# Keys and queries turned by VectorE blocks and SBUF transfers instead of TensorE transposes

## The chip, the cores and the metric

The kernel runs on one core of a Trainium2 chip. Its time is the device time of one execution in microseconds, from runs of the whole program. A profiled execution gives a trace beside it: busy times of the engines, what each instruction waited for, and the transfers.

## What is computed

A gated linear recurrence (4 batches, 8 heads, 768 steps, head dimension 48) is followed by a feed-forward block (3072 tokens, 384 to 2048 to 384). Cut to what matters:

```python
# attention: complex gate, real keys, values and queries
mag = np.sqrt(a_re * a_re + a_im * a_im)
scale = np.minimum(mag, 0.999) / (mag + 1e-06)
ar, ai = a_re * scale, a_im * scale
for t in range(S):
    S_re, S_im = (ar[t] * S_re - ai[t] * S_im + outer(k[t], v[t]),
                  ar[t] * S_im + ai[t] * S_re)
    y[t] = q[t] @ S_re
# feed-forward on x = y with heads side by side
h = x @ w_in
sp = np.maximum(h, 0.0) + np.log1p(np.exp(-np.abs(h)))
out = (h * erf(sp)) @ w_out
```

## The kernel before, in words

The 3072 tokens are cut into twelve units of 256 tokens, three to a batch, and each unit into two chunks of 128 tokens. Tokens lie over the 128 partitions. The path that runs is `quotient_path`; a second one, `product_path`, follows only where a check at the end finds a value out of its limits.

For each unit, the gate work (`g_mag` to `g_sin`, mostly ScalarE activations and VectorE arithmetic) makes running decays `pr` and angles `CS`. With these, `prep` multiplies a chunk's keys and queries by their decay and by cosine and sine: the tiles `kt` and `qt`, 128 tokens by 8 heads by 96 numbers (real and imaginary part of 48). The recurrence inside a chunk then becomes matrix products:

- `cols` (line 996) turns `kt` and `qt`, so that the 96 numbers lie over the partitions and tokens along the row. Four heads at a time are transposed on TensorE (line 1001) into PSUM, and a copy (line 1004) by ScalarE or VectorE brings them to SBUF as `kT` and `qT`. A chunk takes 16 transposes and 4 copies.
- `scores` (line 1008) multiplies turned keys by turned queries, a product of 96 by 128 by 128 for each head, and masks the result to the tile `A`.
- `state` (line 1019) makes the state for the next chunk from `kt`, not turned, and the values.
- `xT` (line 1038) adds, for each head, `A` times values and turned queries times the state (line 1060), four blocks of 32 columns side by side.

The result, turned already, goes into the feed-forward block: `ff_in` (line 1080), the activations `softplus` (line 726) and `erf_times_h` (lines 1107 to 1111), and `ff_out_8` or `ff_out_7` (lines 1140 and 1178).

Each engine works off one queue in program order. The order is written by hand: every step has a due time in units in the table `WHEN`, all steps of all units stand in one list `plan`, and the list is sorted by due time and emitted. So the work of one unit's attention stands between matmuls of the unit before it. Ten numbers, `st`, place the ten steps of a chunk. All transfers of this part but two are issued on SyncE's queue, SP: loads of gates, keys, queries and values, the weights, the outputs, and small ones that carry a row (`wrow` and `w` in `g_decay`, a row of `F` in `g_angle`). An issue on SP waits there for what its transfer needs, and later issues wait behind it.

Tiles come from pools with a set number of buffers: `kT` has two, `qT` three, `kt` and `qt` one each. A tile with one buffer is written again only when its last reader is done.

Of the kernel before, what the change touches and what calls it, by code (L numbers as in the profile page):

```python
# [35 lines left out]
def weave(*streams):  # L36
# [5 lines left out]
    for _, _, _, step in sorted(order, key=lambda e: e[:3]):  # L42
# [1 line left out]

WHEN = {'qact': 3,
 'a00': [0.385, 0.699, 0.3, 0.31, 0.32, 0.33, 0.569, 0.34, 0.35, 0.63],
 'a01': [0.526, 0.422, 0.611, 0.637, 0.649, 0.542, 0.659, 0.66, 0.67, 0.681],
 'n': [0.676, 0.782, 0.769, 0.972, 1.105, 1.183, 1.312, 1.472, 1.61, 1.914, 1.96, 2.139, 2.151, 2.632, 2.395],  # L50
 'g1': [0.702, 0.752, 0.792, 0.802, 0.835, 0.842, 0.873],
 'att': {1: [[0.931, 1.297], 1.089], 2: [[1.716, 2.133], 1.029], 3: [[3.038, 3.627], 1.205]},
 'gate': {2: [1.212, 1.259, 1.372, 1.391, 1.423, 1.442, 1.362], 3: [1.508, 1.606, 1.912, 2.106, 2.59, 2.234, 2.172]},
 'hps': {0: [[0.767, 0.876], [1.01, 1.426]],
         1: [[1.778, 2.017], [2.342, 2.684]],
         2: [[3.136, 3.262], [3.538, 3.868]],
         11: [[11.97, 12.371], [12.438, 12.72]]},
 'act': {0: [2.6, 2.924],
         1: [3.328, 3.7],
         2: [4.148, 4.4],  # L60
         3: [4.9, 5.2],
         4: [5.752, 6.098],
         10: [11.679, 12.031],
         11: [12.456, 12.882]},
 'ops': {0: [3.021, 3.377, 3.704],
         1: [4.001, 4.639, 4.84],
         2: [4.452, 4.798, 4.884],
# [1 line left out]
         10: [12.146, 12.41, 13.01],  # L69
         11: [12.97, 13.469, 14.216]},  # L70
 'T': 5.125,
 'gr': [-1.569, -1.419, -1.119, -0.953, -0.478, -0.129, -1.279],
 'st': [0.014, 0.03, 0.059, 0.09, 0.12, 0.15, 0.206, 0.25, 0.281, 0.388],
 'hr': [1.113, 1.509, 1.573, 1.938],
 'ar': [1.472, 1.947],
 'or': [2.163, 2.683, 3.173],
# [4 lines left out]
 'rest': 12.3,  # L81
 'ok': 13.7,
 'al': [[11.145, 11.515], [11.266, 11.738]],
 'qone': 0,
 'c1g': [0.36, 0.37, 0.38],
 'warm': 0.335}

# [526 lines left out]
def quotient_path(  # L614
# [62 lines left out]
    make_identity(nc, ident)  # L677
    triu = const.tile([P, P], FP, name="triu")
    make_upper_triangular(nc, triu, val=1.0, diag=True)
    cold = tmp.tile([P, P], FP, tag="m", name="cold")  # L680
    vector.memset(cold, 0.0)
    ones = const.tile([P, 1], FP, name="ones")
    vector.memset(ones, 1.0)
# [201 lines left out]
    def g_mag(u, cc=ALL):  # L885

        ar, ai = gate(u, cc)
        s, y = t_("s", cc), t_("y", cc)
        T["s", u] = T["s"]
        i = u * C + cc[0]  # L890
        T["kept"] = u == 1
        act(out=s, in_=ar, func=AF.Square, accum_out=large[:, i:i + 1])
        act(out=y, in_=ai, func=AF.Square)
        T["kept"] = False
        vector.tensor_tensor(out=s, in0=s, in1=y, op=OP.add)
# [14 lines left out]
    def g_log(u, cc=ALL):  # L910
        s, y = T["s"][:, cc[0]:cc[1]], T["y"][:, cc[0]:cc[1]]
        act(out=s, in_=s, func=AF.Ln)
        act(out=y, in_=s, func=AF.Exp, scale=-0.5)
        act(out=y, in_=y, func=AF.Ln, scale=EPS, bias=1.0)
        vector.tensor_scalar(out=s, in0=s, scalar1=0.5, scalar2=math.log(CAP), op0=OP.mult, op1=OP.min)
        T["logs"] = vector.tensor_tensor(out=g_("lr", u, cc), in0=s, in1=y, op=OP.subtract)

    def g_turn(u, cc=ALL):
        th = T["th", u][:, cc[0]:cc[1]]
# [2 lines left out]
    def g_angle(u, c):  # L922

        th = T["th", u][:, c, :]
        goes_on = u % PER > 0 or c > 0
        on_pe = u < PER
        if goes_on:
            prev = T["F", u][:, c - 1, :] if c > 0 else T["F", u - 1][:, C - 1, :]
            if not on_pe:
                row = T["s", u][0:1, c, :]  # L930
                nc.sync.dma_start(out=row, in_=prev[P - 1:P, :])
                vector.scalar_tensor_tensor(out=th[0:1, :], in0=row, scalar=TAU, in1=th[0:1, :],
                                               op0=OP.mult, op1=OP.add)
        ps = ps_b.tile([P, DM], FP, tag="b", name="sum")
        nc.tensor.matmul(out=ps, lhsT=turns, rhs=th, start=True, stop=not (goes_on and on_pe))
        if goes_on and on_pe:
            nc.tensor.matmul(out=ps, lhsT=ident[:, P - 1:P].to_broadcast([P, P]), rhs=prev, start=False, stop=True)
        F = g_("F", u, (c, c + 1))[:, 0, :]
        vector.tensor_scalar(out=F, in0=ps, scalar1=MAGIC, scalar2=MAGIC, op0=OP.add, op1=OP.subtract)
        vector.tensor_tensor(out=F, in0=ps, in1=F, op=OP.subtract)  # L940
# [40 lines left out]
    def chunk(u, c):  # L981
# [5 lines left out]
        def prep(nm, e):  # L987
# [5 lines left out]
                st[nm] = t  # L993
            return f

        def cols(nm, g):
            def f():
                pool, tag = (ps_h, "ff") if (nm, u, c) == ("q", 0, 0) else (ps_a, "a")
                ps = pool.tile([P, HG, P], FP, tag=tag, name="tr")
                for j in range(HG):  # L1000
                    nc.tensor.transpose(out=ps[0:D2, j, :], in_=st[nm][:, g * HG + j].rearrange("p u d -> p (u d)"),  # L1001
                                        identity=ident)
                t = att2.tile([P, HG, P], FP, tag=f"{nm}T", name=f"{nm}T", bufs=2 if nm == "k" else 3)
                (vector.tensor_copy if (nm == "k" if (u, c) == (0, 0) else nm == "q" and u >= WHEN["qact"] and g >= WHEN["qone"]) else scalar.copy)(out=t[0:D2], in_=ps[0:D2])  # L1004
                st[nm, g] = T["cols", nm, g] = t
            return f

        def scores(g):
            def f():
                ps = ps_a.tile([P, HG, P], FP, tag="a", name="sc")  # L1010
                for j in range(HG):
                    nc.tensor.matmul(out=ps[:, j, :], lhsT=st["k", g][0:D2, j, :], rhs=st["q", g][0:D2, j, :],  # L1012
                                     start=True, stop=True)
                A = att2.tile([P, HG, P], FP, tag="A", name="A")
                vector.tensor_tensor(out=A, in0=ps, in1=triu.unsqueeze(1).to_broadcast([P, HG, P]), op=OP.mult)  # L1015
                st["A", g] = A
            return f
# [20 lines left out]
        def xT():  # L1038
# [6 lines left out]
            for i in range(KD):  # L1045
                for b in range(P // QUAD):
# [5 lines left out]
                    for e, lo in parts:  # L1052
                        g, k_ = divmod(2 * pair + e, HG)
                        todo.append((T["v", u][:, c, pair, lo:lo + QUAD], st["A", g][:, k_, :]))
                        if not first:
                            todo.append((T["S"][0:D2, pair, lo:lo + QUAD], st["q", g][0:D2, k_, :]))
                    steps[b] += [(i, lhsT, rhs, n == 0, n == len(todo) - 1) for n, (lhsT, rhs) in enumerate(todo)]
            for turn in zip(*steps):
                for b, (i, lhsT, rhs, start, stop) in enumerate(turn):
# [2 lines left out]
            if not last:  # L1062
                T["S"] = st["S"]
            scalar.copy(out=T["xT", u][:, :, c * P:(c + 1) * P], in_=ps)  # L1064

        return [prep("k", 1), prep("q", 0), cols("k", 0), cols("k", 1), cols("q", 0), cols("q", 1), state, scores(0),
                scores(1), xT]

# [229 lines left out]
        wt[j][0]()  # L1298

    plan = list(zip(WHEN["a00"][4:], first[4:])) + list(zip(WHEN["a01"], chunk(0, 1)))  # L1300
    plan += [(WHEN["warm"], lambda: warm(WARM[5], T["cols", "k", 1][0:D2, 0]))]
    plan += [(0.60, partial(load_qkv, 1))] + [(0.605, wt[j][0]) for j in (6, 7)]
    plan += [(WHEN["n"][j - 1], wt[j][1]) for j in range(2, 16)]
    plan += [(WHEN["n"][5] + 0.001 * j, wt[j][0]) for j in (8, 9)] + [(WHEN["n"][j - 1] + 0.001, wt[j + 2][0]) for j in range(8, 14)]
# [15 lines left out]
    for u in range(NU):  # L1320
        if u > 0:
            begins, spread = WHEN["att"].get(u, ((u, u + WHEN["c1"]), 1.0))
            for c in range(C):
                plan += [(begins[c] + p * spread, f) for p, f in zip(STEPS, chunk(u, c))]
            plan += [(u - 0.38, partial(load_qkv, u))] if u > 1 else []
        if u > 1:
            mag, log, turn, angle, decay, sin, get = WHEN["gate"].get(
                u, [u + x for x in WHEN["gr"]])
# [86 lines left out]
```

## Time and profile before

| | us |
|---|---|
| median of three runs | 723.15 |
| lowest and highest of the three | 721.3 and 723.63 |
| span of the profiled execution, first to last instruction | 719.8 |
| TensorE matmuls busy in it | 699.2 |
| ScalarE busy | 590.1 |
| VectorE busy | 577.8 |

For the profiled execution only its span is on the page, and no time around it. Busy time is the time in which at least one instruction of the engine was running; the shares on the page are of the span. PE is TensorE with its matmuls, PEld its weight loads, DVE is VectorE, ACT is ScalarE, SP is SyncE's queue of transfers. A group's "idle before" is time in which its engine had nothing to run just before it, with the engine and line that ended most of that wait. Float32 matmuls stand twice in the counts, transposes once: 384 matmul instructions are 192 scores, but 384 transposes.

### The profile page before, as it was taken

The numbers are of one execution on the slowest core, as the hardware profiler recorded it, in microseconds if no ns is written. First come the engines' busy times: TensorE is split into PE (matmuls) and PEld (weight loads), VectorE is DVE, ScalarE is ACT, GpSimd is POOL, SyncE is SP. The second block draws the span as 40 slices with busy tenths as digits, with TensorE's granted clock in tenths as the row PEclk, the third lists the DMA queues.
The fourth block names the chain that finished last, engine by engine and source line by source line (L and its number), as shares of the span: only waits on it lengthen the run. The fifth ranks groups of instructions, "written<-read, shape, count | busy, mean of one in ns | idle before, by whom it ended". The sixth has DMA issues, their size and how long they took to land.

```text
span 719.8 us, 12612 instructions
## 1 busy us (share of the span) xinstructions
PE 699.2 (97%) x5048; PEld 595.8 (83%) x5048; DVE 577.8 (80%) x1001; ACT 590.1 (82%) x767; POOL 1.1 (0%) x8
## 2 busy tenths in 40 slices
PE   9899999899999999999999999999999999999996
PEld 8778788767777678988988988997898799899985
DVE  6868985877598789979799799799799896776562
ACT  7879969979988998799699799798797797656860
POOL 0000000000000000000000000000000000000000
PEclk9999999999999999999999999999999999999999
DMA  9886874021302312503233233233331500200000
GB/s 216 222 186 131 200 202 100 1 45 34 56 8 50 66 34 53 136 24 67 87 68 67 88 56 73 94 56 67 99 78 45 132 2 22 89 1 23 0 24 27
DMA packets 156012, 54.50 MB, mean 76 GB/s; under 512 B 142612, under 2 KB 145704, under 8 KB 155944
## 3 DMA queue, kind: packets, MB, share of 16 engines
q1 hardware_dynamic: 153864, 53.22, 31.6%
q8 instruction: 41, 0.67, 0.4%
q10 hardware_dynamic: 2080, 0.39, 0.3%
q14 instruction: 27, 0.22, 0.1%
HBM read 48.82 MB, written 4.75 MB: 74 GB/s over the span
## 4 chain that ended last, share of the span: by engine, by line
ACT 37%; PE 29%; DVE 26%; DMA 5%; issue 3%; SPq 0%; ACTq 0%
PE hps L1080 10%; ACT L725 8%; ACT yy L726 8%; ACT z L726 8%; PE ops L1140 4%; DVE z L1108 4%; DVE yy L1109 4%; DVE e L1110 4%; DVE h L1111 3%; PE ops L1178 3%; ACT e L726 3%; DMA again<-in_moe_w_out_dram 2%; PE tr L1001 2%; PE sc L1012 2%; ACT h L1082 2%
## 5 line engine op out<-in xcount | busy, mean ns | idle before, releaser
L1080 PE MATMUL hps<-xT,w_in_sb 128*128 128x256 f32 x1152 | 270.6, 381 | 2.1 <-ACT xT L1064 1.4
L1080 PEld LDWEIGHTS hps<-xT,w_in_sb 128*128 128x128 f32 x1152 | 212.8, 190 | 36.3 <-ACT xT L1064 2.6
L725 ACT ACT_TABLE_LOAD x90 | 115.5, 1283 | 1.4
L1108 DVE TENSOR_TENSOR z<-z,yy 128x512 f32<-128x512 f32 x96 | 62.9, 684 | 41.0 <-ACT e L726 40.6
L726 ACT ACTIVATE e<-z 128x512 f32<-128x512 f32 x96 | 57.6, 626 | 32.4 <-DVE h L1111 32.0
L1082 ACT COPY h<-hps 128x512 f32<-128x512 f32 x96 | 55.1, 576 | 35.0 <-PE hps L1080 34.8
L1140 PE MATMUL ops<-w_out_sb,h 128*128 128x384 f32 x224 | 77.0, 488 | 0.6 <-DVE h L1111 0.4
L1178 PE MATMUL ops<-w_out_sb,h 128*128 128x192 f32 x384 | 70.9, 327 | 0.1
L1178 PEld LDWEIGHTS ops<-w_out_sb,h 128*128 128x128 f32 x384 | 63.7, 190 | 1.8 <-DVE o L1189 0.5
L1140 PEld LDWEIGHTS ops<-w_out_sb,h 128*128 128x128 f32 x224 | 41.6, 190 | 26.7 <-DVE h L1111 1.5
L1109 DVE SCALAR_TENSOR_TENSOR yy<-z,yy 128x512 f32<-128x512 f32 x96 | 62.8, 682 | 0.4
L1110 DVE TENSOR_TENSOR e<-e,yy 128x512 f32<-128x512 f32 x96 | 62.7, 681 | 0.2
L1111 DVE SCALAR_TENSOR_TENSOR h<-e,h 128x512 f32<-128x512 f32 x96 | 62.7, 681 | 0.2
L726 ACT ACTIVATE z<-h 128x2048 f32<-128x2048 f32 x24 | 45.9, 1912 | 15.2 <-DVE seen L774 11.4
L1012 PE MATMUL sc<-qT,kT 96*128 96x128 f32 x384 | 51.0, 279 | 0.6 <-DVE qT L1004 0.3
L1012 PEld LDWEIGHTS sc<-qT,kT 96*128 96x128 f32 x384 | 47.4, 192 | 4.2 <-DVE qT L1004 1.6
L1178 PE MATMUL ops<-T,S 128*128 128x192 f32 x256 | 47.7, 328 | 0.0
L726 ACT ACTIVATE yy<-z 128x2048 f32<-128x2048 f32 x24 | 45.9, 1912 | 0.4
L726 ACT ACTIVATE z<-z 128x2048 f32<-128x2048 f32 x24 | 45.9, 1911 | 0.4
L726 ACT ACTIVATE yy<-yy 128x2048 f32<-128x2048 f32 x24 | 45.9, 1912 | 0.3
L1178 PEld LDWEIGHTS ops<-T,S 128*128 128x128 f32 x256 | 42.1, 190 | 2.6 <-DVE S L1192 0.3
L1015 DVE TENSOR_TENSOR A<-sc,triu 128x512 f32<-128x512 f32 x48 | 32.4, 682 | 11.9 <-PE sc L1012 11.4
(129 smaller groups left out, 1043.4 us busy)
## 6 DMA issues: line engine op xcount, KB each, us to landing
raw<-in_moe_w_in_dram SPq DMA_DIRECT2D x8, 768.0 KB
raw<-in_moe_w_out_dram SPq DMA_DIRECT2D x8, 768.0 KB
again<-in_moe_w_in_dram SPq DMA_DIRECT2D x8, 768.0 KB
ar<-in_a_re_dram SPq DMA_DIRECT2D x24, 192.0 KB
k<-in_k_dram SPq DMA_DIRECT2D x24, 192.0 KB
q<-in_q_dram SPq DMA_DIRECT2D x24, 192.0 KB
v<-in_v_dram SPq DMA_DIRECT2D x48, 96.0 KB
out_dram<-o SPq DMA_DIRECT2D x24, 192.0 KB
```

The lines of the kernel that those rows point to most:

```text
L725: in_order(scalar.preload_act_table_set(sets[0]))
L726: in_order(scalar.activation(func=func, **kw))
L1012: nc.tensor.matmul(out=ps[:, j, :], lhsT=st["k", g][0:D2, j, :], rhs=st["q", g][0:D2, j, :], start=True, stop=True)
L1015: vector.tensor_tensor(out=A, in0=ps, in1=triu.unsqueeze(1).to_broadcast([P, HG, P]), op=OP.mult)
L1080: nc.tensor.matmul(out=ps[:, e, :], lhsT=w_in_sb[:, kd, f0:f0 + P], rhs=T["xT", u][:, kd, :], start=(kd == 0), stop=(kd == KD - 1))
L1082: scalar.copy(out=T["h", u, sl][:, i:i + 2, :], in_=ps)
L1108: vector.tensor_tensor(out=z, in0=z, in1=y, op=OP.mult)
L1109: vector.scalar_tensor_tensor(out=y, in0=z, scalar=-2.0, in1=y, op0=OP.add, op1=OP.mult)
L1110: vector.tensor_tensor(out=e, in0=e, in1=y, op=OP.mult)
L1111: vector.scalar_tensor_tensor(out=h, in0=e, scalar=1.0 / RT2, in1=h, op0=OP.add, op1=OP.mult)
L1140: nc.tensor.matmul(out=ps, lhsT=lhsT, rhs=w_out_sb[:, i, :], start=i == HALF, stop=i == KF - 1)
L1178: ins = nc.tensor.matmul(out=ps, lhsT=a(sl)[:, i], rhs=b(sl, i), start=sl == 0 and i == 0, stop=sl == NSL - 1 and i == HALF - 1)
```

## The change

From unit one on (the second of the twelve) both chunks of a unit turn keys and queries in another way. VectorE transposes `kt` and `qt` within blocks of 32 by 32 into a tile `X`; one instruction treats all heads of a chunk's keys, another those of its queries. A block then holds the right numbers, but on the partitions of its tokens. Twelve SBUF transfers a chunk, on SP, move blocks of 32 tokens and 32 numbers to the partitions where they belong in a tile `KQ`. `KQ` holds keys and queries of all heads with the head innermost, so a run of 2 KB moves as one piece, and the numbers of one head lie 64 bytes apart. Scores and `xT` read `KQ` with that step through `head`. `X` and `KQ` have one buffer each. Unit zero keeps its transposes on TensorE, and its copies write into `KQ`.

`prep` and the block transposes of a chunk stand sooner, 0.14 unit ahead of the chunk's begin (0.08 for the first chunk of unit one), and much of the gate work and the loads of keys, queries and values (0.60 instead of 0.38 of a unit ahead) moves with them. The logarithms of the decay stay in the tile `s` instead of a tile of their own, the carried row of `F` goes through `y`, and `cold` comes from another pool.

```diff
 WHEN (cut)
- 'att': {1: [[0.931, 1.297], 1.089], ...
+ 'att': {1: [[0.931, 1.355], 1.0], ...
- 'gr': [-1.569, -1.419, -1.119, -0.953, -0.478, -0.129, -1.279],
- 'st': [0.014, 0.03, 0.059, 0.09, 0.12, 0.15, 0.206, 0.25, 0.281, 0.388],
+ 'gr': [-1.443, -1.419, -1.119, -0.953, -0.6, -0.27, -1.279],
+ 'st': [0.206, 0.25, 0.281, 0.388],
+ 'lead': {0: -0.14, (1, 0): -0.08},
+ 'turn': [0.0, 0.015, 0.02, 0.03],
+ 'lq': -0.6,
...
 g_log
-        T["logs"] = vector.tensor_tensor(out=g_("lr", u, cc), in0=s, in1=y, op=OP.subtract)
+        vector.tensor_tensor(out=s, in0=s, in1=y, op=OP.subtract)
...
 chunk
+        def columns():
+            T["KQ"] = st["KQ"] = att2.tile([P, P, 2 * H], FP, tag="KQ", name="KQ", bufs=1)
...
         def cols(nm, g):
...
-                t = att2.tile([P, HG, P], FP, tag=f"{nm}T", name=f"{nm}T", bufs=2 if nm == "k" else 3)
-                (vector.tensor_copy if (...) else scalar.copy)(out=t[0:D2], in_=ps[0:D2])
-                st[nm, g] = T["cols", nm, g] = t
+                i = "kq".index(nm) * H + g * HG
+                t = st["KQ"][0:D2, :, i:i + HG].rearrange("p t h -> p h t")
+                (vector.tensor_copy if nm == "k" and c == 0 else scalar.copy)(out=t, in_=ps[0:D2])
...
+        def turn(nm):
+            def f():
+                if nm == "k":
+                    T["X"] = att1.tile([P, D2 // QUAD, QUAD, 2 * H], FP, tag="X", name="X")
+                src = st[nm].rearrange("p h u d -> p h (u d)").rearrange("p h (b d) -> p b h d", d=QUAD)
+                i = "kq".index(nm) * H
+                vector.transpose(out=T["X"][:, :, :, i:i + H].rearrange("p b t h -> p b h t"), in_=src)
+                if nm == "k":
+                    return
+                columns()
+                for i in range(P // QUAD):
+                    at = slice(i * QUAD, (i + 1) * QUAD)
+                    for b in range(D2 // QUAD):
+                        nc.sync.dma_start(out=st["KQ"][b * QUAD:(b + 1) * QUAD, at], in_=T["X"][at, b])
+            return f
+
+        def head(nm, h):
+            return st["KQ"][0:D2, :, "kq".index(nm) * H + h]
...
 scores
-                    nc.tensor.matmul(out=ps[:, j, :], lhsT=st["k", g][0:D2, j, :], rhs=st["q", g][0:D2, j, :],
+                    nc.tensor.matmul(out=ps[:, j, :], lhsT=head("k", g * HG + j), rhs=head("q", g * HG + j),
...
 xT
-                            todo.append((T["S"][0:D2, pair, lo:lo + QUAD], st["q", g][0:D2, k_, :]))
+                            todo.append((T["S"][0:D2, pair, lo:lo + QUAD], head("q", 2 * pair + e)))
...
+        if u > 0:
+            return [prep("k", 1), prep("q", 0), turn("k"), turn("q"), state, scores(0), scores(1), xT]
...
 plan
-                plan += [(begins[c] + p * spread, f) for p, f in zip(STEPS, chunk(u, c))]
-            plan += [(u - 0.38, partial(load_qkv, u))] if u > 1 else []
+                lead = WHEN["lead"].get((u, c), WHEN["lead"][0])
+                at_ = [begins[c] + lead + p for p in WHEN["turn"]] + [begins[c] + p * spread for p in STEPS]
+                plan += list(zip(at_, chunk(u, c)))
+            plan += [(u + WHEN["lq"], partial(load_qkv, u))] if u > 1 else []
```

The due times of the gate work of units three and four and of a few steps of unit zero differ as well.

## The prediction

> **What bounds the kernel now.** I read the page from part 1 to part 4, then cut the span into stages, because shares of a whole span hide where each engine has room. First part 1, and the shares by engine of the chain that ended last (part 4):
> ```profile
> span 719.8 us, 12612 instructions
> ...
> PE 699.2 (97%) x5048; PEld 595.8 (83%) x5048; DVE 577.8 (80%) x1001; ACT 590.1 (82%) x767; POOL 1.1 (0%) x8
> ...
> ACT 37%; PE 29%; DVE 26%; DMA 5%; issue 3%; SPq 0%; ACTq 0%
> ```
> The reader is to see two things that pull against each other. TensorE is busy 97% of the time, so work taken from it can shorten the span; but the chain runs over ScalarE and VectorE for 63% of its length, so they follow closely behind. Four stages (columns: stretch, its length, then busy us and instruction count of PE, PEld, DVE, ACT, POOL; granted clock; DMA share; GB/s):
> ```profile
> 0.00:120.00 120.00, 113.78 (x962) 95.84 (x963) 97.87 (x167) 99.75 (x169) 1.08 (x8) 1.00 0.81 187
> 120.00:240.00 120.00, 117.33 (x682) 86.51 (x682) 87.77 (x148) 107.67 (x133) 0.00 (x0) 1.00 0.18 33
> 240.00:540.00 300.00, 295.95 (x2227) 259.56 (x2226) 264.78 (x456) 266.49 (x334) 0.00 (x0) 1.00 0.31 72
> 540.00:720.00 180.00, 172.19 (x1182) 153.92 (x1180) 127.41 (x233) 116.18 (x134) 0.00 (x0) 0.99 0.12 36
> ```
> The first stage is also bound by loads (DMA share 0.81). From 120 us to 660 us TensorE leads; in the third stage DVE and ACT stand at 88 and 89% behind it. The groups that the change touches, kept apart by form (busy us, mean ns | idle before):
> ```profile
> L1012 PE MATMUL sc<-qT,kT 96*128 96x128 f32 x384 | 51.0, 279 | 0.6 <-DVE qT L1004 0.3 <-ACT qT L1004 0.2
> L1060 PE MATMUL y<-qT,S 96*32 96x128 f32 x640 | 33.8, 272 | 0.0
> L1001 PE MATMUL tr<-ident,qt 128*96 128x128 f32 x192 | 27.1, 275 | 2.3 <-DVE qt L992 1.2 <-ACT kT L1004 1.0
> L1001 PE MATMUL tr<-ident,kt 128*96 128x128 f32 x192 | 26.1, 275 | 4.4 <-DVE kt L992 4.1
> L1004 ACT COPY kT<-tr 96x512 f32<-96x512 f32 x46 | 24.9, 574 | 5.0 <-PE tr L1001 4.9
> L1004 DVE COPY qT<-tr 96x512 f32<-96x512 f32 x36 | 24.1, 679 | 2.1 <-PE tr L1001 1.9
> L992 DVE TENSOR_TENSOR qt<-qr,CS 128x768 f32<-128x768 f32 x23 | 21.8, 948 | 0.1
> L1004 ACT COPY qT<-tr 96x512 f32<-96x512 f32 x12 | 6.9, 578 | 0.4 <-PE tr L1001 0.4
> ```
> Matmuls overlap, so a group's cost to TensorE is its busy time over its count, not the mean of one: (27.1+26.1)/384 = 0.138 us for a transpose.
>
> [...] This bears on the change, whose operands have a step of 64 bytes. No matmul and no VectorE group of the trace of before has that step, so its price stays open.
>
> **The change part by part.**
> *TensorE.* 22 chunks (units one to eleven, two each) lose 16 transposes: 352 x 0.138 = 48.5 us, 699.2 to 650.7. Of it 8.9 us lies in the first stage (64 of its 96 transposes; unit zero's 32 stay), 8.8 in the second, 21.6 in the third, 9.1 in the last, by the same stretches for L1001 alone.
> *Evacuations.* ACT loses 44 copies of k and 8 of q, 52 x 0.575 = 29.9 us; its order in the changed program also holds 7 table loads fewer, 7 x 1.283 = 9.0. ACT: 590.1 to 551.2. DVE loses the 36 copies of q, 24.1 us. Unit zero's eight copies stay, now writing at the 64-byte step.
> *Block transposes.* DVE gains 44 of 128x768. Lower bound the 948 ns of L992, upper bound twice that, if the strided write pays. I take 0.95: +41.8 us, DVE 577.8 + 41.8 - 24.1 = 595.5. They stand between `prep` and the gate work, so what follows on DVE (the four multiplies of `erf_times_h`, which ACT waits for) starts up to 1.9 us later per chunk; in the second and fourth stages DVE's room (27 and 29%) covers that, in the third hardly.
> *SBUF transfers.* 12 a chunk, 264 more issues on SP. Small issues last 0.26 to 0.46 us each (wrow and w rows), so 12 are about 5.5 us of SP's time, and the last lands some 1.2 us later (SP's wait for wrow: 8.7 us in 7 times; longest 3.3). About 7 us, up to 9. Queued behind them on SP are loads for a later unit, the wrow/w rows, the carried row of F and output stores; each can come one burst later, 5.5 us, and SP has most of its time free. The first of each burst waits for DVE's last transpose and for TensorE's last read of the one KQ buffer; the next scores wait for all 12. With the changed order of TensorE and the durations of before, the work between that last read and those scores is 9 to 39 us over the 22 chunks, under 11 in three of them: mostly hidden, and I charge 3 us. If the cover were gone in every chunk, 22 x 7 = 154 us would lie open. 17.3 MB more over 700 us raise the mean of 76 GB/s to about 102; the first stage moves 187, so it is not the limit except there.
> *Strided reads.* Scores read both operands, and y one, with 64 bytes between elements: 51.0 + 33.8 = 84.8 us of TensorE. Lower bound no cost (a score takes 51.0/384 = 0.133 us for 128 columns, about one column a nanosecond, a slow stream that may absorb it); upper bound doubled, +84.8. I take none, with less certainty than anything else here.
> *Moved.* `prep` stands 0.14 unit (about 8 us) sooner, gate work and loads of q, k, v (from -0.38 to -0.6) move likewise: no instruction is added, but gates must be ready sooner; loads have landed early in the third stage (DMA share 0.31), so nothing, bounded by 2 us either way. One tile for `lr` less and `cold` in another pool: nothing; both lie off every wait shown.
>
> **The sum.** First stage: loads bind, a third of 8.9, 3 us. Second: 7 of 8.8, ACT being relieved at once. Third: TensorE needs 296.0 - 21.6 = 274.4, DVE 264.8 + 20 x 0.95 - 13.3 = 270.5; two engines within 4 us of each other don't interlock perfectly, so I take 283 instead of 300: 17. Last: 7 of 9.1, the tail after the last scores being unchanged. 34 less 3 for late transfers is 31 us. From the span 719.8: 688.8. The page gives no time around the span of that execution; the median of the runs, 723.15, is 3.35 above the span, which I carry: **692 us**. About 0.3%, 2 us, is what a measurement here can tell from no change.
>
> **The rivals.**
> *(1) As summed*, chance 0.42: 672 to 702. For it: the 97%, and that both helpers of TensorE together lose work.
> *(2) VectorE becomes the bound*: strided writes make a transpose 1.9 us; third stage DVE 264.8 + 38 - 13.3 = 289.5, which runs at 294 or so: 6 us instead of 17, and 5 less elsewhere, about 708. [...] Chance 0.19, range 702 to 719.
> *(3) No change*, chance 0.05: [...]: 721 to 725.
> *(4) Slower by strided reads on TensorE.* The place is the scores and y. It decides from 48.5/84.8 = +57% on; doubled, 84.8 - 48.5 = 36 us more: 759. At +80% it is 742. For it: [...] TensorE has no room to hide it. Against it: the slow float32 stream. Chance 0.34, range 726 to 765.
> *(5) The change doesn't do what it says*: the changed order shows 352 transposes gone and 264 transfers added, so this is excluded.
>
> **The numbers.** Faster 0.42 + 0.19 = 0.61, same 0.05, slower 0.34. The range for 8 in 10 reaches from 668 (all 48.5 us gained, and the 2.3 + 4.4 us that TensorE sat idle before transposes: 723.15 - 55.2) to 750, leaving out strided reads beyond +90%. The likeliest case's own range is 672 to 702.
>
> **What would show it.** Right: no rows tr but unit zero's 32; PE busy near 651; sc and y<-KQ near 51 and 34 us; transposes X<-kt and X<-qt near 950 ns; scores waiting for KQ's transfers under 5 us in all. Wrong: sc above 0.2 us each, transposes near 1.9 us, or a large wait of PE for the transfers to KQ.

## The result, and the profile after

The changed kernel takes 807.5 us (median of four runs, 806.2 to 811.8) against 722.2 for the kernel before: 1.119 times as long, 95% interval 1.116 to 1.123. The prediction was 692 us, and faster. Its range ended at 750.

First the page of the changed kernel, part 1 and the shares of the chain that ended last:
```profile
PE 747.6 (92%) x4696; PEld 630.1 (78%) x4696; DVE 614.3 (76%) x1009; ACT 563.2 (70%) x708; POOL 1.1 (0%) x8
...
PE 70%; DVE 14%; ACT 11%; issue 2%; SPq 1%; DMA 1%; DVEq 0%; ACTq 0%
```
The count of TensorE's instructions fell by 352, as foreseen, but its busy time rose from 699.2 to 747.6 us. Beside that its idle time grew from 20.6 (719.8 less 699.2) to 62.5 us (810.1, the span, less 747.6). The chain now lies on TensorE for 70% of its length, 29% before. ScalarE is busy 26.9 us less than before, VectorE 36.5 us more. The four stages (stretch, length, then busy us and count of PE, PEld, DVE, ACT, POOL; granted clock; DMA share; GB/s):
```profile
0.00:120.00 120.00, 102.28 (x668) 85.42 (x669) 88.68 (x148) 77.40 (x129) 1.08 (x8) 0.84 0.69 157
120.00:240.00 120.00, 107.30 (x607) 80.90 (x606) 74.50 (x109) 82.27 (x102) 0.00 (x0) 0.90 0.42 91
240.00:540.00 300.00, 281.29 (x1762) 234.98 (x1761) 251.12 (x412) 226.06 (x274) 0.00 (x0) 0.95 0.36 82
540.00:810.10 270.10, 256.73 (x1665) 228.80 (x1663) 199.98 (x342) 177.50 (x205) 0.00 (x0) 0.99 0.25 64
```
The column after POOL is new to the story. The granted TensorE clock, which stood at 1.00, 1.00, 1.00 and 0.99 before, is 0.84 to 0.99 now. Over the span it is 0.938 instead of 0.998. The groups that the change touches, by form (busy us, mean ns | idle before):
```profile
L1034 PE MATMUL sc<-KQ 96*128 96x128 f32 x384 | 88.7, 395 | 1.0 <-DMA KQ<-X 0.9
...
L1082 PE MATMUL y<-KQ,S 96*32 96x128 f32 x640 | 54.0, 401 | 0.0
...
L1017 DVE STREAM_TRANSPOSE X<-kt 128x768 f32<-128x768 f32 x22 | 32.8, 1491 | 3.1 <-DMA y<-F 2.3 <-DMA KQ<-X 0.7
L1017 DVE STREAM_TRANSPOSE X<-qt 128x768 f32<-128x768 f32 x22 | 32.6, 1481 | 0.0
...
L1007 ACT COPY KQ<-tr 96x512 f32<-96x512 f32 x6 | 5.8, 1036 | 1.2 <-PE tr L1003 1.2
```
Scores and the products with the state went from 84.8 to 142.7 us (88.7 + 54.0). Everything that reads or writes the 64-byte step is slower by half or more: a score's record takes 0.231 instead of 0.133 us, a `y` record 0.084 instead of 0.053, ScalarE's copy 1036 instead of 574 ns, a block transpose 1491 and 1481 ns where one with a contiguous write takes 950 (`m_prices` below). The scores hardly wait for the transfers (0.9 us). Waits of TensorE, by what ended them (us in total, times, longest):
```profile
PE y L1082 <- ACT pr L723: 7.2, 2, 4.9
PE sum L932 <- DVE th L929: 7.1, 4, 3.1
PE y L1082 <- DVE A L1037: 6.1, 2, 4.0
PE ops L1202 <- DVE o L1213: 6.0, 1, 6.0
```
They are few and long, and none of them names the new work. The wait for `o` is an example of what follows a long one. Two stretches around it, columns as above:
```profile
445.00:450.00 5.00, 0.00 (x0) 0.00 (x0) 5.00 (x6) 4.93 (x5) 0.00 (x0) 0.72 0.00 0
450.00:455.00 5.00, 4.38 (x15) 3.95 (x16) 1.92 (x5) 4.94 (x5) 0.00 (x0) 0.60 0.32 77
```
VectorE is full for 5 us with the multiplies of `prep`, two sums of `ff_out_7` and both block transposes (the last 2.6 us, from 447.56 us on), which stand ahead of `o` in its queue. TensorE does nothing meanwhile, and over the 5 us afterwards it is granted 0.60 of its clock: the clock stood at 0.50 from 447.2 us, 2.5 us into the wait, to 454.0 us, 3.4 us after the wait's end.

From the span before, the sum to the span after is

719.8 - 48.5 (transposes) + 60.7 (steps in reads, from `k_cols` below) + 41.9 (more idle time of TensorE) + 36.2 (rest of its busy time) = 810.1 us.

The 36.2 us are what is left over, and not measured by themselves. Of this the lower clock explains most. The stretches in which the clock stood at 0.50, added up:
```profile
sum 100.06, PE 72.26 PEld 56.48 DVE 76.22 ACT 64.97 POOL 0.00; mean PE 5.16 PEld 4.03 DVE 5.44 ACT 4.64 POOL 0.00
```
TensorE was busy for 72.3 of these 100.1 us, and for 16.8 of them with reads of `KQ`, which take as long at either clock (0.211 and 0.214 us in `m_prices` below). Other matmuls don't: in these stretches an `ops` record of line 1202 took 0.351 us (13.35 us for 38) and an `hps` record of line 1104 0.402 (19.29 for 48), outside them 0.176 and 0.231. If the other 55.4 us would have been shorter by the same shares, 0.50 and 0.43, that is an estimate of 24 to 28 us; some 8 to 12 us stay without a name. The readings suggest two causes, the layout, and waits that lower the clock. The experiments take them in turn.

### The profile page after: what moved, and what is told of

It is laid out like the page before. It is cut to its first block, busy times and chain, and to the rows that moved or that the text cites. A ratio compares the mean times of both kernels' runs of the same rounds, so it can differ in the third digit from the quotient of the medians.

```text
span 810.1 us, 12259 instructions
## 1 busy us (share of the span) xinstructions
PE 747.6 (92%) x4696; PEld 630.1 (78%) x4696; DVE 614.3 (76%) x1009; ACT 563.2 (70%) x708; POOL 1.1 (0%) x8
## 4 chain that ended last, share of the span: by engine, by line
PE 70%; DVE 14%; ACT 11%; issue 2%; SPq 1%; DMA 1%; DVEq 0%; ACTq 0%
PE hps L1104 24%; PE ops L1202 16%; PE sc L1034 9%; PE ops L1164 7%; PE y L1082 6%; DVE X L1017 3%; PE kv L1046 2%; ACT L722 2%; PE sum L932 2%; ACT yy L723 2%; PE sum L949 1%; ACT z L723 1%; DVE e L1134 1%; DVE yy L1133 1%; DVE z L1132 1%
## 5 line engine op out<-in xcount | busy, mean ns | idle before, releaser
L1104 PE MATMUL hps<-xT,w_in_sb 128*128 128x256 f32 x1152 | 276.1, 391 | 10.4 <-DVE w_in_sb L800 5.5
L1104 PEld LDWEIGHTS hps<-xT,w_in_sb 128*128 128x128 f32 x1152 | 222.5, 196 | 51.1 <-ACT xT L1086 6.5
L722 ACT ACT_TABLE_LOAD x83 | 106.5, 1283 | 1.3
L1034 PE MATMUL sc<-KQ 96*128 96x128 f32 x384 | 88.7, 395 | 1.0 <-DMA KQ<-X 0.9
L1034 PEld LDWEIGHTS sc<-KQ 96*128 96x128 f32 x384 | 85.8, 306 | 2.6 <-issue 2.0
L1202 PEld LDWEIGHTS ops<-w_out_sb,h 128*128 128x128 f32 x384 | 66.9, 197 | 8.9 <-DVE o L1213 6.4
L1164 PEld LDWEIGHTS ops<-w_out_sb,h 128*128 128x128 f32 x224 | 43.5, 196 | 31.7 <-DVE o L1172 2.8
L1134 DVE TENSOR_TENSOR e<-e,yy 128x512 f32<-128x512 f32 x96 | 62.5, 682 | 0.1
L1202 PE MATMUL ops<-T,S 128*128 128x192 f32 x256 | 52.2, 345 | 8.7 <-DVE S L1216 4.3
L1082 PE MATMUL y<-A,v 128*32 128x128 f32 x768 | 46.6, 299 | 13.3 <-ACT pr L723 7.2
L1202 PEld LDWEIGHTS ops<-T,S 128*128 128x128 f32 x256 | 45.9, 201 | 12.2 <-DVE S L1216 5.0
L1082 PE MATMUL y<-KQ,S 96*32 96x128 f32 x640 | 54.0, 401 | 0.0
L1082 PEld LDWEIGHTS y<-A,v 128*32 128x32 f32 x768 | 28.0, 124 | 32.1 <-ACT pr L723 8.8
```

Source lines behind the costliest of these rows:

```text
L722: in_order(scalar.preload_act_table_set(sets[0]))
L1034: nc.tensor.matmul(out=ps[:, j, :], lhsT=head("k", g * HG + j), rhs=head("q", g * HG + j), start=True, stop=True)
L1082: nc.tensor.matmul(out=ps[b * QUAD:(b + 1) * QUAD, i, :], lhsT=lhsT, rhs=rhs, start=start, stop=stop)
L1104: nc.tensor.matmul(out=ps[:, e, :], lhsT=w_in_sb[:, kd, f0:f0 + P], rhs=T["xT", u][:, kd, :], start=(kd == 0), stop=(kd == KD - 1))
L1134: vector.tensor_tensor(out=e, in0=e, in1=y, op=OP.mult)
L1164: nc.tensor.matmul(out=ps, lhsT=lhsT, rhs=w_out_sb[:, i, :], start=i == HALF, stop=i == KF - 1)
```

## The experiments

The theories are these, as the expectations number them: (1) the 64-byte step makes TensorE's reads slow; (2) it makes VectorE's block transposes slow; (3) multiplies and block transposes, put sooner into VectorE's queue, hold up what TensorE waits for; (4) the transfers do it, by their place on SP's queue, their bytes or their landing. A fifth came later: (5) the instruction order that is built around the transfers. The diffs show only the lines that matter.

### The layout

`m_prices` measures single operations, 48 matmuls a row. It was executed once. Its calls, shortened:
```diff
+ matmul(out, lhsT=KQ1[0:96, i, :],  rhs=KQ1[0:96, j, :])    # steps of 4 bytes, line 42
+ matmul(out, lhsT=KQ16[0:96, :, i], rhs=KQ1[0:96, j, :])    # weights at 64 bytes, line 46
+ ...                                                        # 16 bytes line 62, 8 bytes line 66
```


> Not the kernel's computation at all: rows of equal instructions for their prices, then q copied to the output. Float32 matmuls 96x128 by 96x128 with weights and moving operand at steps of 4, 8, 16, 32 and 64 bytes, block transposes of 128x768 with writes at 64, 32 and 4 bytes, evacuations of 96x512 with writes at 64 and 4 bytes, and the twelve transfers of a chunk with runs of 2048, 512 and 128 bytes. Theory 1: with both operands at 64 bytes a matmul costs 0.2 us or more of TensorE's time instead of 0.13, at full clock; most of it at 16 bytes already. If the clock alone made the rows slow, all steps cost the same. Theory 2: the transpose with a contiguous write takes 0.95 us and with 64 bytes 1.49; the other way, all take 1.49. Transfers: 2048-byte runs about 7 us from first issue to last landing, 128-byte runs two to four times that.

Groups by form in its trace:
```profile
L62 PE MATMUL w4m<-KQ 96*128 96x128 f32 x96 | 22.8, 417 | 0.0
...
L46 PE MATMUL w16m<-KQ,KQ 96*128 96x128 f32 x96 | 21.2, 412 | 0.0
...
L66 PE MATMUL w2m<-KQ 96*128 96x128 f32 x96 | 13.0, 302 | 0.0
L42 PE MATMUL w1m<-KQ 96*128 96x128 f32 x96 | 10.9, 275 | 0.0
...
L89 DVE STREAM_TRANSPOSE X<-kt 128x768 f32<-128x768 f32 x6 | 8.7, 1452 | 0.0
L91 DVE STREAM_TRANSPOSE X<-kt 128x768 f32<-128x768 f32 x6 | 5.7, 950 | 0.0
```
Busy time over count is the price of one record, and a float32 matmul has two (96 records for the 48 matmuls of a row). It is 0.114 us with steps of 4 bytes, 0.238 with 16, 0.221 with 64 in the weights alone (0.220 in the moving operand alone, 0.219 in both). A transpose takes 950 ns with a contiguous write and 1452 with the 64-byte step (1554 at 32 bytes); the evacuations take 617 against 1007 ns on ScalarE and 661 against 1008 on VectorE. The twelve transfers of a chunk take 7.55, 7.78 and 8.00 us to issue with runs of 2048, 512 and 128 bytes, and land 2.0 us after.

The clock has to be watched beside these prices. The contiguous row ran at 1.00, those with 16 bytes and more at 0.50 for most of their length, without a gap between instructions. But the first of them, line 46, began at the full clock. This line alone in two stretches (length, then PE and PEld; clock; DMA share; GB/s):
```profile
33.20:38.90 5.70, 5.70 (x27) 5.70 (x28) 1.00 0.01 3
39.10:53.00 13.90, 13.90 (x65) 13.90 (x66) 0.50 0.00 0
```
That is 0.211 us for a record at the full clock and 0.214 at half: the step is dear by itself, and at the step the clock makes no difference. With 8 bytes it does: line 66 took 3.40 us for 17 records at 0.50 and then 9.10 us for 79 at 1.00, which is 0.115, the price without a step; its mean of 0.135 comes from the clock. So the jump lies between 8 and 16 bytes, 0.115 against 0.238 us.

The next two runs show the price in a whole kernel, at nearly the same clock in both. `c_sched` is the kernel before with the change's due times, contiguous `kT` and `qT`; `k_cols` has the layout of the change for all units, TensorE's transposes, and neither block transposes nor transfers.
```diff
 c_sched (from before)
-                plan += [(begins[c] + p * spread, f) for p, f in zip(STEPS, chunk(u, c))]
+                at_ = [begins[c] + lead + p for p in WHEN["turn"][:2]] + [begins[c] + p * spread for p in STEPS]
+                plan += list(zip(at_, chunk(u, c)))     # and the changed gr, gate, att, lq
 k_cols (from the changed kernel)
-        if u > 0:
+        if u > NU:
             return [prep("k", 1), prep("q", 0), turn("k"), turn("q"), ...
```


> The kernel before with only the due times of the change: both multiplies of a chunk 0.14 unit sooner, the gate work and the loads of q, k and v at the changed kernel's times; the transposes stay on TensorE, no block transpose, no transfer, no strided read. Theory 3 (order): most of the added idle time of TensorE (42 us) appears here too, and the time is 745 to 765 us. Theory 1 and theory 2 (strided reads, slow block transposes): no change but a few us, 718 to 728. If the sooner preparation alone is good, 715 or less.

> The changed kernel with all chunks made as unit zero: TensorE's transposes, copies from PSUM to KQ at the 64-byte step, strided reads; no block transpose and no transfer. With the kernel before at the change's due times (732.2 us, TensorE's transposes and contiguous tiles) it isolates the layout. Theory 1: 52 us of strided reads on a TensorE that is 96% busy, and 96 copies of 1.03 instead of 0.575 to 0.68 us, on ACT most: 785 to 815 us, as slow as the changed kernel although nothing is moved off TensorE. If the layout matters little and block transposes with transfers made the loss: 735 to 755.

`c_sched` took 732.2 us, `k_cols` 788.6. TensorE's line of part 1 of each, and the scores of `k_cols`:
```profile
PE 704.7 (96%) x5048; PEld 600.9 (82%) x5048; DVE 575.1 (79%) x1001; ACT 581.3 (80%) x760; POOL 1.1 (0%) x8
```
```profile
PE 765.4 (97%) x5048; PEld 650.6 (83%) x5048; DVE 576.3 (73%) x987; ACT 616.8 (78%) x774; POOL 1.1 (0%) x8
...
L1034 PE MATMUL sc<-KQ 96*128 96x128 f32 x384 | 92.9, 400 | 1.9 <-ACT KQ L1007 1.9
```
Clocks are 0.987 and 0.985, idle times 26.4 and 21.4 us. The same number of instructions costs TensorE 60.7 us more, and the time grows by 56.4. ScalarE is busy 35.5 us more too, mostly by copies to the step, but TensorE idles less than in `c_sched`, so it is TensorE's reads that bind. The orders of the two differ as well. With the price from `m_prices` this shows theory 1: the layout takes back more than the 48.5 us of the transposes, before anything is moved.

`a_pe_contig` leaves the changed kernel as it is, its instruction order too, and only gives TensorE other addresses to read. It leaves out the right scores of six heads in eight.
```diff
         def head(nm, h):
+            if h not in (0, H - 1):
+                return w_in_sb[0:D2, 0, "kq".index(nm) * P:("kq".index(nm) + 1) * P]
```


> The changed kernel, but TensorE reads the keys and queries of heads 1 to 6 from a contiguous 96x128 piece of w_in_sb; only heads 0 and 7 are still read from KQ with 64 bytes between elements, so that every wait for KQ stays. It leaves out the right scores of six heads in eight. Block transposes, their transfers and the order of the work are those of the changed kernel. Theory 1 (strided reads on TensorE): 288 of 384 scores go back from 0.231 to 0.133 us and 480 of 640 y products from 0.084 to 0.053 us, together 43 us less TensorE time; the time falls from 807 to about 764 us. Theory 3 (the sooner preparation blocks VectorE's queue and TensorE waits): TensorE's busy time falls, its idle time of 62 us stays or grows, the granted clock stays near 0.94, and the time falls by less than 15 us, to 793 or more. Theory 2 (the block transposes with strided writes, 1.49 us each, bind): no change.

```profile
PE 708.6 (91%) x4696; PEld 600.3 (77%) x4696; DVE 612.5 (79%) x1009; ACT 562.0 (72%) x708; POOL 1.1 (0%) x8
```
TensorE's busy time fell by 39.0 us, to 708.6 (43 expected), the time by 28.1 to 779.4. Idle time is not less (68.3 against 62.5 us), and the clock is hardly higher (0.945 against 0.938). So both causes are at work: the layout gives 28 us for three quarters of the reads, and the waits and the low clock are there without them.

### Due times

`c_sched` says that the sooner due times alone cost some 10 us (722.9 to 732.2, ratio 1.010 to 1.016). `g_due` takes them out of the changed kernel.
```diff
-                at_ = [begins[c] + lead + p for p in WHEN["turn"]] + [begins[c] + p * spread for p in STEPS]
+                at_ = [begins[c] + p * spread for p in WHEN["turn"] + STEPS]     # turn: 0.014, 0.03, 0.059, 0.12; the old gr, gate, att, ...
```


> The changed kernel with the due times of the kernel before: multiplies, block transposes and transfers of a chunk stand where the multiplies and TensorE's transposes stood, the gate work and loads too (unit zero's second chunk alone keeps the changed order of its copies). Strided reads, block transposes and transfers stay. Theory 3: the added idle time goes, the granted clock returns to 0.99, and the time is 722 plus (58 of strided reads less 48.5 of transposes), 730 to 740 us. Theory 1 alone: TensorE stays the bound with the same work, no change from 807 us by more than 10. Theory 4 (transfers on SP are hidden only by the sooner preparation): slower than 807, with waits of the scores for DMA of some 5 us in each of 22 chunks, 830 to 900.

It took 803.9 us, with 61.6 us idle. So the sooner due times are not what the waits come from. The rest of theory 3, that the block transposes themselves hold up VectorE's queue wherever they stand, is not tested by this.

### The transfers, or what is built around them

`n_nodma` leaves the 264 transfers out; `p_pool` issues them on GpSimd; `t_tiny` cuts them to 512 bytes; `d_noturn` keeps them and drops 42 of 44 block transposes; `l_late` starts the change with unit three.
```diff
 n_nodma
-                columns()
-                        nc.sync.dma_start(out=st["KQ"][b * QUAD:(b + 1) * QUAD, at], in_=T["X"][at, b])
+                st["KQ"] = T["KQ"]
 p_pool
+                        nc.gpsimd.dma_start(out=st["KQ"][b * QUAD:(b + 1) * QUAD, at], in_=T["X"][at, b])
 t_tiny
+                        nc.sync.dma_start(out=st["KQ"][b * QUAD:(b + 1) * QUAD, i * QUAD, 0:4], in_=T["X"][at, b, 0, 0:4])
 d_noturn
+                if (u, c) == (1, 0):
                     vector.transpose(...)
 l_late
+        if u > 2:
             return [prep("k", 1), prep("q", 0), turn("k"), turn("q"), ...
```


> The changed kernel without its 264 transfers: the block transposes are made, but from unit one on the scores read the KQ that unit zero left; it leaves out the moving of the blocks, so that the right keys and queries never arrive. Theory 4 (SP's queue: the twelve issues wait for VectorE's X, and the weights, gates and q, k, v behind them come late; and the 17 MB compete with the loads): of the 47 us lost by the second xT copy of unit two, 25 or more come back, and the time is 760 to 780 us. Theory 3 (VectorE's own queue): the transfers don't matter, 795 or more. Strided reads stay in both.

> The changed kernel with the twelve transfers of a chunk issued by GpSimd instead of SP, so that no load and no store stands behind them. Theory 4 in its form 'order on SP's queue': 770 to 790 us, much as without transfers. Theory 4 in its form 'bytes compete with the loads': no change from 807. Theory 3: no change. Issues by GpSimd may each be dearer; then the scores wait for KQ and it is slower than 807.

> The changed kernel with its 264 transfers cut to 512 bytes each (32 rows of 16 bytes) in place of 64 KB: the same issues on SP in the same place, waiting for the same X and the same last reads of KQ; it leaves out nearly all the moving of the blocks. Without any transfer the time was 759.7 us, with the issues on GpSimd 786.9. If what costs is SP standing still before them (order), this run stays at 795 to 808. If it is their bytes beside the loads, it falls to 760 to 775. GpSimd's run says about 21 us for the place on SP and 27 for the rest, which would make it 775 to 790.

> The changed kernel with the block transposes of its first such chunk alone: X is then kept and 42 of 44 transposes are gone (62 us of VectorE's time); the transfers go on, waiting for KQ's last reads only; it leaves out the right keys and queries. Theory 3 (VectorE's in-order queue): 62 us less in a queue that TensorE waits on; and SP no longer waits for X. 760 to 780 us. If the transfers cost by their bytes alone and VectorE has room: 795 or more.

> The changed kernel with units one and two made as unit zero: TensorE's transposes and strided copies to KQ for six chunks, block transposes and transfers from unit three on (18 chunks). Due times and strided reads as in the changed kernel. The changed kernel is 47 us behind the kernel before by the second xT copy of unit two; with the due times alone it is 8 us behind there. If block transposes and transfers make the rest of it, this run is at most 20 us behind at that point and ends at 770 to 785 us. If strided reads and strided copies make it (in unit zero alone they lose 7 us), it is still 35 or more behind and ends at 795 to 815.

The runs took 759.7 us without transfers, 786.9 on GpSimd, 809.6 with 512 bytes, 772.3 without block transposes and 783.3 with the change from unit three on. `l_late` stood 20.8 us behind the kernel before at the second `xT` copy of unit two, about as expected, where the changed kernel stood 46.7. I read GpSimd's run as the cost of SP's queue, 21 us, and what `n_nodma` gained beyond it, 27 us, as the rest of the transfers. `t_tiny` contradicts the second: with next to no bytes it gained nothing.

What they have in common I saw only then. The account of the kernel ahead of the prediction leaves something out: due times only rank the instructions. Each engine's final order comes out only when the program is built, and an edit elsewhere can change it. Of TensorE's 2364 instructions in the main part (a float32 matmul counted once), 1753 stand in another place in `n_nodma` than in the changed kernel, 1375 in `t_tiny`, 654 in `p_pool`, none in `a_pe_contig`. Counted from the order in the traces, the numbers come within 3% of these; the 159 places that the expectation of `f_pool` names for `p_pool` are too few. The scores of the first chunk of unit eight stand behind 342 `hps` matmuls in the kernel before, 360 in the changed kernel, 342 in `n_nodma`.

A first test kept the scores at their old place and the first multiply of the erf part behind the masking (`o_pin`).
```diff
+    def behind(ins, nm="sc"):
+        tc.add_manual_dep(ins.ins, T[nm].ins.name, order, reason="behind the scores")
...
+                        behind(nc.tensor.matmul(out=ps[:, e, :], lhsT=w_in_sb[:, kd, f0:f0 + P], ...
```


> The changed kernel, but each hps and ops matmul that comes after a chunk's scores by due time is also kept behind them on TensorE, and each first erf multiply behind the masking of A on VectorE. In the kernels as built, the scores of chunk (8,0) stand behind 342 hps matmuls before, 360 in the changed kernel, 342 without transfers and 372 in the contiguous version; here they stand behind 342 again. Transfers stay real and on SP. Theory 5 (the transfers cost by the order that is built around them: scores stand up to 18 matmuls later, then A, y and xT, which ACT and VectorE wait for): 765 to 785 us. If the transfers cost by waits on the chip (SP's queue, the landing): TensorE now stands at the scores, waits of the scores for DMA of 3 us or more in most of 22 chunks, 805 to 840.

It took 814.2 us. Waits of TensorE:
```profile
PE sum L935 <- DVE th L932: 19.9, 2, 18.8
PE sc L1037 <- DMA y<-F: 11.4, 2, 7.1
```
With some instructions held, others moved and made waits of their own, so this told nothing apart. The last two runs therefore hold every instruction of TensorE, VectorE and ScalarE exactly in the changed kernel's order and alter only the transfers: `f_nodma` has none, `f_pool` issues them on GpSimd.
```diff
+    for engine, turns_ in ORDER.items():        # PE, DVE, ACT: the changed kernel's order, as numbers
+        own = [i for i in traced if str(i.engine).endswith("." + engine)]
+        for a, b in zip(turns_, turns_[1:]):
+            tc.add_manual_dep(own[b], own[a].name, order, reason="as in the other program")
```


> The changed kernel without its 264 transfers, as before (KQ stays what unit zero left, so the right keys and queries never arrive), but with every instruction of TensorE, VectorE and ACT in exactly the changed kernel's order; without transfers and with an order of its own the time was 759.7 us. Theory 5 (the order built around the transfers is what costs): no gain left, 795 to 808 us. Theory 4 (the transfers' issues, waits and landing on the chip cost): 755 to 770 us, as without them before. In between, each has its share.

> The changed kernel with the transfers issued by GpSimd and every instruction of TensorE, VectorE and ACT in exactly the changed kernel's order; with an order of its own (which differed in 159, 193 and 33 places) GpSimd's version took 786.9 us. If SP's queue costs: 785 to 795 us again. If those 21 us were the few differences of order: 803 to 812.

`f_nodma` took 809.7 us (802.8 to 813.8), `f_pool` 813.3 (810.6 to 816.0). Without a single transfer of these, and so without a wait for one, the time of the changed kernel is there in full; what `n_nodma` gained, it gained by its order. GpSimd's 21 us are gone as well once the order is held. Part 1 of `n_nodma` and of `f_nodma`, the same work in two orders:
```profile
PE 723.5 (96%) x4696; PEld 614.6 (82%) x4696; DVE 611.2 (81%) x1009; ACT 562.0 (75%) x708; POOL 1.1 (0%) x8
```
```profile
PE 738.0 (92%) x4696; PEld 624.3 (78%) x4696; DVE 613.8 (77%) x1009; ACT 563.4 (70%) x708; POOL 1.1 (0%) x8
```
TensorE idles for 30.1 against 62.9 us, at a clock of 0.986 against 0.950. And the waits of TensorE in `f_nodma` are those of the changed kernel (its lines are numbered 144 to 148 higher, for the list of the order):
```profile
PE y L1226 <- ACT pr L871: 7.2, 2, 4.9
PE sum L1080 <- DVE th L1077: 7.1, 4, 3.1
PE y L1226 <- DVE A L1181: 6.8, 2, 4.8
...
PE ops L1346 <- DVE o L1357: 5.9, 1, 5.9
```
They are 7.2, 7.1, 6.8 and 5.9 us, where the changed kernel has 7.2, 7.1, 6.1 and 6.0. Theory 4 falls for this order: SP's queue, the bytes and the landing cost nothing beyond the spread of these runs. Theory 5, the order, is shown to be worth 50 us between these two orders. Three things stay open. Which of the displaced instructions matter is not known. The order of `n_nodma` was not run with the transfers, so it is not shown that the changed kernel could have it. And no run drops the block transposes in a held order (`d_noturn`, and `l_late` with fewer of them, have orders of their own), so their own share in the waits is not known; in the wait for `o` they are 2.6 of 6.0 us.

### Towards a better version

`e_contig` lays `KQ` and `X` out with the head outside the row, so that nothing has a step and the transfers move runs of 128 bytes. `v_mix` adds GpSimd's transfers and the late start to it. `o_contig`, `o_contig_pool` and `o_mix` add the held scores of `o_pin` to it, to it with GpSimd's transfers, and to `v_mix`.
```diff
-            T["KQ"] = st["KQ"] = att2.tile([P, P, 2 * H], FP, tag="KQ", name="KQ", bufs=1)
+            T["KQ"] = st["KQ"] = att2.tile([P, 2 * H, P], FP, tag="KQ", name="KQ", bufs=1)
-                vector.transpose(out=T["X"][:, :, :, i:i + H].rearrange("p b t h -> p b h t"), in_=src)
+                vector.transpose(out=T["X"][:, :, i:i + H, :], in_=src)
```


> The changed kernel with the head outside the row in KQ and X, so that every score and y product reads 96x128 without a step, and block transposes and unit zero's copies write without one; the twelve transfers of a chunk then move runs of 128 bytes instead of 2048. Everything else as in the changed kernel. Theory 1 (strided reads): TensorE's busy time falls by 52 us (a_pe_contig: 39 for three quarters). Theory 2 (strided writes): 44 transposes fall from 1.49 to 0.95 us, 24 us of VectorE's time. Together, by theories 1 and 2, 807 falls to 745 to 755 us: a_pe_contig's 28 us for three quarters make 37, and VectorE's 24 us less wait another 15 to 25. Theory 3 (the longer queue and the waits bind whatever the layout): 770 or more. If 128-byte runs are dear beside the loads, slower than a_pe_contig's 779; the table of transfers (8.0 us a burst against 7.6) says no.

> A correct version put together from what helped: contiguous KQ and X (52 us less TensorE time, 24 us less VectorE time), transfers issued by GpSimd, block transposes from unit three on only. If the gains add up (807 less 21 for GpSimd, less 24 for the late start, less about 37 for reads without a step): 725 to 735 us, about the kernel before. If TensorE, relieved, waits for the other engines as it did in the contiguous version (112 us idle): 770 to 800. [...]

> The contiguous version (820.5 us) with the same order kept: scores behind 342 instead of 372 hps matmuls at chunk (8,0). Theory 5: its 112 us of idle time come from the order, and most of them go: 740 to 770 us. If the 128-byte runs themselves land late: the scores wait for DMA, 815 or more.

> The contiguous version with the order kept and the transfers issued by GpSimd. GpSimd brought 21 us in the changed kernel with nearly the same order on the other engines. If that was SP's queue, 15 to 25 us less than the same kernel with the transfers on SP: 720 to 750 us. If the gain there was chance of the order, no difference.

> The version put together before (contiguous, GpSimd's transfers, block transposes from unit three on; 761.7 us) with the order kept. All causes named so far are then taken away but the due times (10 us) and VectorE's 34 us for 36 contiguous block transposes. Adding up: TensorE needs 704.7 less 36/44 of 48.5, 665 us; with 30 us idle and a clock of 0.985: 705 to 725 us, equal to the kernel before or faster. If VectorE and ACT bind (A still stands behind up to eight erf operations more on VectorE): 735 to 760.

They took 820.5, 761.7, 849.6, 848.4 and 812.3 us. Part 1 of `e_contig`:
```profile
PE 706.6 (86%) x4696; PEld 597.0 (73%) x4696; DVE 595.8 (73%) x1009; ACT 561.6 (69%) x708; POOL 1.1 (0%) x8
```
Its transposes are down to 941 to 968 ns and its scores to 54.1 us, as theories 1 and 2 say, which makes 41 us less on TensorE and 18 on VectorE; and yet TensorE idles for 112.2 us at a clock of 0.920. Its largest waits are for `A` (28.7 us in seven times); one wait of scores for the transfers to `KQ` is 9.0 us, so the landing is not free in every order. 1673 of its instructions stand elsewhere than in the changed kernel, scores up to 15 `hps` matmuls later in units eight to eleven. No version here beats the kernel before; the fastest that does the whole computation with block transposes is `v_mix`, 5.4% slower (1.050 to 1.058). That GpSimd's queue changed next to nothing between `o_contig` and `o_contig_pool` agrees with `f_pool`. In the three runs with held scores the wait for `th` that came up in `o_pin` is 41 to 43 us, so they tell more of the holding than of the layout.

## Why the prediction was wrong, step by step

Two terms failed, the strided reads and what was moved, and each was large enough to turn the sign. The layout alone makes `k_cols` 56.4 us slower than `c_sched`, more than the 48.5 us to be gained. And `a_pe_contig`, without the step in three quarters of the reads, still takes 779.4 us, with no less idle time than the changed kernel. If the last quarter is worth a third of the 28.1 us, some 770 us would be left without any step, by this estimate.

- **Transposes.** 352 are gone from TensorE and the 48.5 us with them, which is right as counted. TensorE's busy time, "699.2 to 650.7", ended at 747.6.
- **Strided reads.** "I take none" is the first step that failed. The reads cost 60.7 us of TensorE's busy time in `k_cols`, and in the changed kernel scores and `y` rows take 142.7 us instead of 84.8, +68%, past the +57% that the prediction gave as the point from which it is slower. The reason for taking none, a slow float32 stream that absorbs the step, was wrong: a score's record needed 0.133 us without a step and 0.231 with it. Rival 4 had this mechanism and its point; at +68% it would have read 732 us, and it was priced alone, with a chance of 0.34.
- **Block transposes.** They were taken at 0.95 us, an estimate from the 948 ns of L992, with 1.9 as the upper bound; 1.49 and 1.48 were measured, 23.6 us more in all than taken. The price of L992 fits a contiguous write (0.95 in `m_prices`, 0.94 to 0.97 in `e_contig`) and not one with the step. Rival 2, VectorE as the bound, did not come: VectorE was busy 76%.
- **Evacuations.** Seven table loads fewer (83 of 1283 ns) is right. ScalarE ended at 563.2 instead of 551.2; unit zero's copies at the step, which the text named and did not price, are 2.8 us of the difference.
- **SBUF transfers.** The prediction charged 3 us for lateness and 7 to 9 us for a burst. The scores waited 0.9 us; twelve issues took 7.55 us in `m_prices`, and the last landed 2.0 after. The direct price was about right, and `f_nodma` shows that in this order no time hangs on the transfers.
- **Moved.** "Nothing, bounded by 2 us either way" is the second step that failed. The sooner due times alone are some 10 us (`c_sched`). In the changed kernel TensorE's idle time is 41.9 us more, and the lower clock is another 24 to 28 us by the estimate above; two orders of the same work differ by 32.8 us of idle time (`n_nodma` and `f_nodma`). The sum was made from busy times of an order that the change did not leave in place. I gave the order no cost and no upper bound, and no rival had it.
- **The sum.** The third stage was to take 283 us where TensorE needs 274.4 and VectorE 270.5, and the 27 and 29% of VectorE's room in the second and last stages were read as if they could be used at any moment. They can't, where each engine works off a fixed queue: TensorE waited for `o`, `A`, `S` and `pr` (8.2, 6.1, 8.6 and 7.2 us in all), on engines that were 70 and 76% busy.

## What to carry to other kernels

Price an operand's step before the work that it saves: here the steps of 16 to 64 bytes took a record of a float32 matmul from 0.114 to about 0.22 us or more, a step of 8 bytes cost nothing (0.115 at the full clock), and steps of 32 and 64 bytes took a block transpose from 0.95 to 1.45 us or more. The reads and writes that pay can be more than the operations that are saved. In a kernel whose engines follow a fixed order, an edit is two edits, the work and the order that comes out of it; compare the orders before reading a gain or loss as the price of what was edited, and hold the order fixed in the experiment that decides. A long wait of TensorE can cost twice, once idle and once at a lower clock: at the end of each of the six waits of 4 us or more in the changed kernel, the clock stood at 0.50.

## What was not expected of the hardware

- Reads with the step were followed by a lower clock although TensorE was busy. In `m_prices` it was granted at 0.50 from 39.0 to 144.8 us; the rows with 16 bytes and more ran from 33.0 to 141.3 us without a gap. It fell again at 179.0, 3.5 us after line 78 began to read with the step, and stood at 1.00 in between, for the rows with 8 bytes and without a step. The whole kernels show it in small: in the changed kernel 16 score records ran from 522.26 us on with no wait ahead of them, and the next stretch was granted half the clock with TensorE busy throughout:
```profile
525.70:529.10 3.40, 3.40 (x11) 2.92 (x9) 3.40 (x7) 0.00 (x0) 0.00 (x0) 0.50 0.90 284
```
  `k_cols` has two such places (from 237.5 and from 391.1 us), and over its whole span it loses little by it (0.985, where `c_sched` has 0.987). That the step is the cause is the likeliest reading and was not tested further; why it would be, no run here shows.
- A step of 64 bytes was no dearer than one of 16 (0.219 us with both operands at 64, 0.238 at 16), and one stepped operand cost as much as two.
- The size of SBUF transfers' runs mattered little: 128 bytes instead of 2048 added 6% to a burst's issue time (8.00 against 7.55 us).
